# A fused attention and two-MoE kernel: 2 KB rows for keys and queries, z spread by halves of the rows, items of 592 slots, a new order list

## Chip, core and metric

The kernel runs on one core of a Trainium2 chip. The metric is the device time of one execution in microseconds (us). The times of the kernel before are 625.58, 625.61 and 626.13 us, median 625.61 us. A separate execution was profiled; the rows below are from it.

## What is computed

Three layers follow one another. The inputs are 4 batches of 8 heads, 576 tokens and 64 features a head, so 2304 tokens of 512 features, all in 4-byte floats.

```python
def phi(x):                                  # linear attention, 128 random features
    proj = np.einsum('bhsd,md->bhsm', x, omega)
    h = proj - np.sum(x * x, axis=-1, keepdims=True) / 2.0
    return np.exp(h - np.max(h, axis=-1, keepdims=True)) / np.sqrt(m)
kv = np.einsum('bhsm,bhsd->bhmd', k_p, v)
z = np.sum(k_p, axis=2)
x = np.einsum('bhsm,bhmd->bhsd', q_p, kv) / (np.einsum('bhsm,bhm->bhs', q_p, z)[..., None] + 1e-06)

h = x @ w_in                                 # layer two: softmax-gated unit, layer norm
solu = h * softmax(h)
x = (solu - mean) / np.sqrt(var + 1e-06) * g_ln @ w_out

e_idx = np.argmax(x @ w_gate, axis=1)        # layer three: one of 8 experts a token
for e in range(8):
    mask = e_idx == e
    ye = np.maximum(x[mask] @ w1[e], 0.0) @ w2[e]
    out[mask] = gate_w[mask, None] * eom[mask, e, None] * ye
```

## The kernel before, in words

A token tile is 128 tokens, so there are 18 tiles. Products that must be precise are made of three: each operand is split into an upper and a lower part, and `mm3` multiplies upper by upper, upper by lower and lower by upper (L162).

The first two layers are one long list of small steps, `ORDER`. Each entry is a step's name and its index, and `in_order` (L905) traces them one after the other and ties each instruction to the one before it on its engine. So the list fixes the order on PE, DVE, ACT, POOL and SP, and an engine that waits holds everything behind it. A second list, `LOADS`, gives the order of the loads on the SP queue; `pump` (L243) issues the next load as soon as its ring of buffers has room. The steps that matter here:

- `da` to `dl` turn a 512-column piece of `w_in` or `w_out`, stored in 8 bytes a number, into upper and lower parts: `db`, `dc`, `dd`, `de`, `df` on DVE, `dp` and `dg` on POOL, `dh` on ACT, and `dl` (L313) on DVE again, which takes the upper part from the number.
- `kp`, `kx`, `ke` are the projection of a key tile on PE, its maxima on DVE and its exponentials on ACT; `qp`, `qx`, `qe` are the same for queries. A projection holds two of the four half banks called `big` until its exponentials are done.
- `kv` and `kw` add a key tile to the sums of its batch. `vz` (L465) spreads the sums z of a batch over all partitions with four products, `zp`; `qz`, `qr` and `qs` divide by the denominators, `qz` and `qs` as long instructions on POOL.
- `ha`, `hb` (L162, tile `h`) are the products of the second layer, `u` and `l` (tile `x`) those with `w_out`; they need all of `dl`. `lo` (L643) stores a finished tile to DRAM (`x2d`).
- `wu` are products of ones with ones whose result nobody reads.
- `re`, `rg`, `rh` give each token a place in its expert's list, and `zb`, `zg`, `zt` pick and gather the first 256 tokens of the first expert. `zl` and `zm` (L869) load that expert's two weights on the SP queue, 2 MB each.

The third layer cuts each expert's tokens into items of at most `CAP` slots, in blocks of 128. Four items always run (`NSURE`); a fifth and more run only if the counts ask for them (`n_items`). `up` (L947) makes the hidden products (tile `hp`) with the slots as moving columns: 256 and then `CAP - 256` for the first item, two halves of `CAP // 2` for the others. `down` (L969) makes the output products (tile `yp`), 512 moving columns each, with up to 128 slots as the stationary side. Each block is scaled, scattered to `out_y` by POOL, and the next item's blocks are gathered and turned in between (`xpose`, L856).

Of the kernel before, what the change touches and what calls it, by code (L numbers as in the profile page):

```python
# [63 lines left out]
def slots(j):  # L64
# [15 lines left out]
    qe0 dc6 kv6 kv7 db7 dc7 dd7 dp0 ke11 dh0 dd6 de6 df6 dp11 vz0 dg11 de7 vy0 dl0 kp9 kx9 vt0 vd0 wu1 kp14 kx14 da3  # L80
    ke9 qz0 df7 kv8 vc1 qr0 db3 ke14 qp1 qx1 dc3 dp7 dh7 dl7 qe1 kv9 kv10 da8 dd3 de3 qp2 qx2 qs0 qz1 qr1 vz1 vy1 dp6
    kv11 qta0 qe2 qca0 qp5 qx5 dh6 vt1 gc2 gd2 db8 qs1 vd1 kp12 kx12 qe5 qtb0 qcb0 wu1 qta1 qtb1 dc8 nx0 qca1 qcb1
    kp13 ke12 ga3 kv12 dd8 de8 df8 gb3 kx13 ke13 qp4 qz2 qr2 dl6 qx4 dp8 dg8 kv13 gd1 df3 kp15 da4 db4 nx1 kx15 xh0
    dc4 dd4 de4 df4 vc2 qe4 kw13 kp16 kx16 ke15 xl0 xh1 ke16 qz5 kv14 kv15 ga0 kp17 gb0 dp3 dp4 vt2 kv16 dh4 qr5 vd2
    kx17 qp3 dl4 qx3 ke17 da5 db5 ha0 qs2 qz4 qr4 qe3 dh11 qta2 qca2 hxa0 qtb2 xl1 dh3 dl3 dc5 dd5 kv17 qcb2 da15 db15
    dc15 qs5 qta5 qca5 vz2 qz3 ha1 vy2 vc3 vt3 vd3 de5 df5 qr3 dp5 dd15 dh5 dl5 de15 df15 dp15 dg15 nx2 xh2 hxa1 hb1
    hxb1 da14 hb0 qs3 xl2 he1 ma1 hxb0 he0 mz1 ha2 ma0 mz0 dh8 qtb5 qcb5 qta3 qtb3 nx5 hxa2 qs4 dl8 db14 dc14 hb2 mb1
    da13 dd14 de14 hxb2 qca3 qcb3 qta4 nx3 xh5 qca4 he2 df14 dp14 dg14 xh3 xl5 qp6 ma2 qx6 qtb4 qcb4 qe6 db13 dc13
    dd13 de13 df13 ha5 mc1 qp7 qx7 qe7 mb0 hxa5 xl3 hb5 dl11 dp13 dg13 qz7 ta1 hxb5 gc0 gd0 tb1 da12 ca1 sa1 he5 dh14
    ma5 mz5 cb1 nx4 xh4 qp8 qx8 ga5 gb5 gc3 mb5 sb1 gd3 qe8 ta5 ga7 qr7 qs7 gb7 gc5 gd5 xl4 ta0 ca5 sa5 ca0 sa0 ga6  # L90
    gb6 tb5 cb5 sb5 mc5 gc7 qp9 qx9 dh15 qta7 qtb7 qca7 gc6 db12 dc12 dd12 de12 df12 qcb7 qz8 qr8 mc0 md0 ha4 dh13 qe9
    gd6 tb0 gd7 hb4 hxa4 hxb4 cb0 dp12 dg12 ga4 qz6 mz2 mb2 gb4 qr6 dh12 dl12 nx7 xh7 sb0 md1 he4 qs6 ma4 mz4 dl13 gc4
    me1 ha3 hxa3 mc2 qs8 gd4 hb3 hxb3 md5 qta6 qca6 qtb6 dl15 dl14 u1 xl7 he3 ma3 qcb6 nx6 xh6 xl6 qp11 qx11 mz3 ta2
    ca2 me0 mb4 sa2 qta8 qca8 qz9 qr9 ua1 l1 la1 lo1 mb3 ta3 qtb8 qcb8 u0 tb2 ub0 ub1 qe11 ca3 sa3 ua0 qs9 qp12 qx12
# [1085 lines left out]
```

## Time and profile before

| What | Value |
|---|---|
| median of 3 runs | 625.61 us |
| the profiled execution, its own time | 624.91 us |
| its span | 623.1 us |
| PE busy | 601.9 us (97%) |
| DVE busy | 359.5 us (58%) |
| ACT busy | 300.9 us (48%) |
| POOL busy | 236.7 us (38%) |
| HBM read, written | 44.70 MB, 9.70 MB |

PE is the engine of matrix products, DVE and ACT are the vector and scalar engines, POOL is GpSimd, and SP issues loads and stores. A share over the whole span is a mean over stages: DVE is nearly full in the first quarter and nearly idle in the last third. The profiled execution took 1.8 us more than its span, and 0.7 us less than the median.

### The profile page before, as it was taken

Reading aid. Unit: us, or ns where it says so; the run is one execution under the profiler, and the core shown is the slowest. Engines: PE = TensorE matmul, PEld = TensorE weight load, DVE = VectorE, ACT = ScalarE, POOL = GpSimd, SP = SyncE. Lnnn points to the kernel's source line nnn. Section 1 sums busy time; section 2 is a strip of 40 time slices with the busy share of each in tenths; the row PEclk is TensorE's granted clock in tenths of the full one; section 3 lists DMA queues with packets and bytes.
Section 4 is the critical chain, followed back from the end, with each engine's and each line's share of the span. In section 5 each row is a group of like instructions: output and inputs, shape, how many; then the busy total and the mean of one; then the engine's idle time right before and its main releaser. Section 6 shows DMA issues by size and latency. Waiting matters only on the chain.

```text
span 623.1 us, 12619 instructions
## 1 busy us (share of the span) xinstructions
PE 601.9 (97%) x5026; PEld 532.5 (85%) x5026; DVE 359.5 (58%) x952; ACT 300.9 (48%) x743; POOL 236.7 (38%) x169
## 2 busy tenths in 40 slices
PE   9999999998999999999999998999999999999994
PEld 8887888887988898988989897888798899879983
DVE  4998998999555364775676876864223123222200
ACT  5988985794653456345344423324333242325110
POOL 1435685558334226225201111173653182316011
PEclk9999999999999999999999999999999999999998
DMA  9986521210100001000004015066730433000010
GB/s 291 315 271 173 152 100 35 86 35 1 35 18 18 1 35 35 0 36 1 35 1 153 35 52 202 23 185 235 247 136 18 169 108 136 35 34 10 2 50 29
DMA packets 35077, 55.06 MB, mean 88 GB/s; under 512 B 2559, under 2 KB 21375, under 8 KB 35008
## 3 DMA queue, kind: packets, MB, share of 16 engines
q1 hardware_dynamic: 28384, 31.73, 15.6%
q0 software_dynamic: 6336, 22.29, 10.4%
q8 instruction: 42, 0.69, 0.5%
q14 instruction: 27, 0.22, 0.1%
q10 hardware_dynamic: 288, 0.13, 0.1%
HBM read 44.70 MB, written 9.70 MB: 87 GB/s over the span
## 4 chain that ended last, share of the span: by engine, by line
PE 71%; DVE 12%; issue 7%; DMA 6%; POOL 1%; ACT 1%; SPq 0%; POOLq 0%; DVEq 0%; ACTq 0%
PE x L162 14%; PE hp L162 14%; PE h L162 14%; PE yp L162 12%; PE qps L162 3%; PE qT L166 3%; PE lT L166 2%; PE kv L162 2%; PE xT L162 2%; DMA out_y<-y,idxs 2%; DVE kmx L374 1%; DVE w2l L150 1%; DMA xge<-x2d,idxe 1%; DMA kr<-in_kT 1%; PE xT L166 1%
## 5 line engine op out<-in xcount | busy, mean ns | idle before, releaser
L162 PE MATMUL x<-w2h,lth 128*128 128x256 f32 (+1 forms) x288 | 83.6, 290 | 0.8 <-DVE w2l L150 0.4
L162 PE MATMUL x<-w2l,lth 128*128 128x256 f32 (+1 forms) x288 | 82.0, 285 | 1.6 <-DVE w2l L150 1.6
L162 PE MATMUL x<-w2h,ltl 128*128 128x256 f32 (+1 forms) x288 | 81.9, 284 | 0.0
L958 DVE SCALAR_TENSOR_TENSOR htl<-hp,hth 128x304 fp32r<-128x304 f32 (+2 forms) x64 | 30.3, 474 | 82.7 <-ACT hth L957 68.9
L162 PE MATMUL hp<-xth,w1h 128*128 128x304 f32 (+1 forms) x224 | 68.6, 306 | 0.7 <-DVE htl L958 0.7
L162 PE MATMUL hp<-xtl,w1h 128*128 128x304 f32 (+1 forms) x224 | 68.4, 305 | 0.0
L162 PE MATMUL hp<-xth,w1l 128*128 128x304 f32 (+1 forms) x224 | 68.0, 304 | 0.0
L162 PE MATMUL yp<-w2h,hth 128*128 128x512 f32 (+1 forms) x160 | 64.1, 401 | 0.0
L162 PE MATMUL yp<-w2h,htl 128*128 128x512 f32 (+1 forms) x160 | 63.5, 397 | 0.0
L162 PE MATMUL yp<-w2l,hth 128*128 128x512 f32 (+1 forms) x160 | 63.4, 396 | 0.0
L479 POOL TENSOR_TENSOR pz<-qe,zb 128x1024 f32<-128x1024 f32 (+1 forms) x20 | 48.8, 2442 | 30.7 <-ACT qe L381 26.7
L957 ACT ACTIVATE hth<-hp 128x304 fp32r<-128x304 f32 (+2 forms) x64 | 27.2, 424 | 67.6 <-PE hp L162 67.6
L162 PE MATMUL h<-w1h,xth 128*128 128x512 f32 x144 | 58.9, 409 | 0.3 <-ACT qt L504 0.3
L162 PE MATMUL h<-w1h,xtl 128*128 128x512 f32 x144 | 57.0, 396 | 0.4 <-DVE xtl L150 0.4
L162 PE MATMUL h<-w1l,xth 128*128 128x512 f32 x144 | 56.9, 395 | 0.0
L162 PEld LDWEIGHTS x<-w2l,lth 128*128 128x128 f32 x288 | 54.2, 188 | 2.3 <-DVE w2l L150 1.8
L162 PEld LDWEIGHTS x<-w2h,lth 128*128 128x128 f32 x288 | 54.1, 188 | 2.1 <-ACT xo L153 0.8
L162 PEld LDWEIGHTS x<-w2h,ltl 128*128 128x128 f32 x288 | 54.3, 189 | 0.0
L150 DVE TENSOR_TENSOR xtl<-xT,xth 128x512 fp32r<-128x512 f32 (+1 forms) x36 | 24.2, 671 | 50.3 <-ACT xth L863 44.9
L981 POOL DMA_INDIRECT out_y<-y,idxs x20 | 20.1, 1006 | 77.1 <-ACT y L980 75.4
L490 POOL TENSOR_TENSOR qe<-qe,rd 128x1024 f32<-128x1024 f32 x18 | 34.4, 1916 | 35.6 <-DVE rd L486 28.3
L980 ACT ACTIVATE y<-yp,scs 128x512 f32<-128x512 f32 (+1 forms) x20 | 13.8, 688 | 70.3 <-PE yp L162 62.0
(210 smaller groups left out, 1468.6 us busy)
## 6 DMA issues: line engine op xcount, KB each, us to landing
raw<-in_w POOLq DMA_DIRECT2D x12, 1024.0 KB
v<-in_v SPq DMA_DIRECT2D x18, 260.0 KB, 4.7
kr<-in_kT SPq DMA_DIRECT2D x18, 256.0 KB, 5.9
qr<-in_qT SPq DMA_DIRECT2D x18, 256.0 KB, 3.1
x2d<-xo SPq DMA_DIRECT2D x18, 256.0 KB, 2.0
wout<-in_w_out SPq DMA_DIRECT2D x8, 512.0 KB, 4.9
win<-in_w_in SPq DMA_DIRECT2D x8, 512.0 KB, 6.1
raw<-in_w SPq DMA_DIRECT2D x4, 1024.0 KB, 6.2
```

What stands on the lines that cost most here:

```text
L150: return eng.tensor_tensor(out=out_, in0=a, in1=hi.bitcast(F32), op=ALU.subtract)
L162: return in_turn(nc.tensor.matmul(ps, **kw))
L166: return in_turn(nc.tensor.transpose(ps, x, ident[0:k, 0:k]))
L374: nc.vector.tensor_reduce(out=nmx[:, j, :], in_=of[kind, t][j], axis=AX.X, op=ALU.max, negate=True)
L479: nc.gpsimd.tensor_tensor(out=pz[r0:r1], in0=of["qe", t][r0:r1], in1=of["zb", b][r0:r1], op=ALU.mult)
L490: nc.gpsimd.tensor_tensor(out=e3, in0=e3, in1=of.pop(("rd", t)).to_broadcast([P, H, M]), op=ALU.mult)
L957: act = nc.scalar.activation(out=hi, in_=ps[:, 0:n], func=AF.Relu)
L958: dve = nc.vector.scalar_tensor_tensor(out=lo, in0=ps[:, 0:n], scalar=0.0, in1=hi.bitcast(F32), op0=ALU.max, op1=ALU.subtract)
L980: nc.scalar.activation(out=y, in_=ps, func=AF.Copy, scale=scs[0:k, col:col + 1])
L981: nc.gpsimd.indirect_dma_start(out=out, out_offset=bass.IndirectOffsetOnAxis(ap=idxs[0:k, col:col + 1], axis=0), in_=y, in_offset=None, bo ...
```

## The change

Six things change together.

1. Keys and queries are laid out by the host so that a tile is 128 rows of 2048 bytes. Before, a tile was 512 pieces of 512 bytes. Values lose their column of ones, which the sums took from an on-chip tile already: rows of 2048 bytes for 2080.
2. `vz` makes each of its four products from 64 partitions in place of 128, alternately from the lower and the upper half.
3. `CAP` is 592 for 608.
4. The threshold that moves a place into the next item, and the rounding of the place, are written so that they hold for 592.
5. The list `ORDER` is another one, with 2 entries of `wu` (13 products) for 9 entries (36 products).
6. The list `LOADS` is another one.

```diff
-CAP = 608
+CAP = 592
...
 LOADS = [(x[0], int(x[1:])) for x in """
-    k0 w9 k1 k2 w2 k6 k5 w1 v0 c0 w10 k8 k7 k3 v2 k10 q0 k4 v1 w0 w11 k9 v3 w7 v4 w3 q1 v5 w4 v6 w6 k11 k17 k12 v7 w8
+    k1 k0 w9 k4 k3 k2 v0 w10 v2 w2 k8 v1 c0 k6 c1 k10 v3 k9 w6 v4 q0 w3 k5 w11 w7 v5 q1 w0 v6 k11 w4 q5 w1 k7 k12 k14
...
 ORDER = """
-    wu9 wu5 kp0 kx0 da9 ke0 db9 dc9 da2 dd9 wu3 kp1 kx1 de9 df9 wu5 kp2 kx2 ke1 db2 dp9 dg9 ke2 dc2 wu6 kp6 dd2 kv0
+    da9 wu9 wu4 kp1 kx1 ke1 kp0 db9 dc9 kp2 kx0 ke0 kx2 ke2 dd9 da2 de9 da10 df9 kv0 dp9 kp4 kx4 ke4 kp3 kx3 ke3 db10
...
-                r = ap.tile([P, H, D + 1], F32, tag="va", name=f"v{t}", bufs=3)
-                nc.sync.dma_start(out=r, in_=v[t * P:(t + 1) * P])
+                r = ap.tile([P, H * D], F32, tag="va", name=f"v{t}", bufs=3)
             else:
                 r = raw2(f"{kind}r{t}")
-                src = qT if kind == "q" else kT
-                nc.sync.dma_start(out=r.rearrange("p (c t) -> p c t", c=NPAIR),
-                                  in_=src[:, :, t * P:(t + 1) * P].rearrange("c p t -> p c t"))
+            nc.sync.dma_start(out=r, in_=dict(v=v, q=qT, k=kT)[kind][t * P:(t + 1) * P])
+            if kind == "v":
+                r = r.rearrange("p (h d) -> p h d", h=H)
...
-            for i in range(4):
-                mm(pss[i // 2][:, i % 2], lhsT=ident[:, 32 * i:32 * i + 1].to_broadcast([P, P]), rhs=zk[:, b], start=True, stop=True)
+            for i in (0, 2, 1, 3):
+                rows = slice(i // 2 * D, i // 2 * D + D)
+                mm(pss[i // 2][:, i % 2], lhsT=ident[rows, 32 * i:32 * i + 1].to_broadcast([D, P]), rhs=zk[rows, b], start=True, stop=True)
...
-                V.scalar_tensor_tensor(out=place, in0=place, scalar=float(k * (CAP // SHORT + 1) - 1), in1=place,
+                V.scalar_tensor_tensor(out=place, in0=place, scalar=(k * CAP - 0.5) / SHORT + k - 1, in1=place,
...
-            V.tensor_scalar(out=pli, in0=place, scalar1=float(SHORT), scalar2=None, op0=ALU.mult)
+            V.tensor_scalar(out=pli, in0=place, scalar1=float(SHORT), scalar2=0.25, op0=ALU.mult, op1=ALU.add)
```

The lists move instructions on every engine. Three places follow.

The first is DVE's beginning, once the constants are made. `kmx` are the maxima of a key tile (two instructions a tile), `f` is a piece of weights under conversion. Before:

```order
L374 TENSOR_REDUCE kmx_162<-kps_0_150 128x4
L374 TENSOR_REDUCE kmx_162<-kps_1_151 128x4
L271 TENSOR_SCALAR f_165<-f_165 128x512
L276 TENSOR_SCALAR f_165<-f_165 128x512
L282 SCALAR_TENSOR_TENSOR f_165<-wout_113,f_165 128x512
L374 TENSOR_REDUCE kmx_198<-kps_0_184 128x4
L374 TENSOR_REDUCE kmx_198<-kps_1_185 128x4
L287 SCALAR_TENSOR_TENSOR f_165<-wout_113,f_165 128x512
```

Of the change:

```order
L372 TENSOR_REDUCE kmx_166<-kps_0_153 128x4
L372 TENSOR_REDUCE kmx_166<-kps_1_154 128x4
L270 TENSOR_SCALAR f_136<-f_136 128x512
L275 TENSOR_SCALAR f_136<-f_136 128x512
L372 TENSOR_REDUCE kmx_202<-kps_0_178 128x4
L372 TENSOR_REDUCE kmx_202<-kps_1_179 128x4
L372 TENSOR_REDUCE kmx_214<-kps_0_192 128x4
L372 TENSOR_REDUCE kmx_214<-kps_1_193 128x4
L281 SCALAR_TENSOR_TENSOR f_136<-wout_115,f_136 128x512
```

Three key tiles now stand ahead of the third step of the first piece of weights, where one stood.

The second is PE around the first `vz`, with the sums `kv` on one side and projections (`qps`, `kps`) on the other. Before:

```order
L162 MATMUL kv_1_624<-ke_649,v_670 32x128 x8
L162 MATMUL kv_1_624<-ke_649,ones 32x128 x4
L162 MATMUL zp_0_803<-zk,ident 128x256 x2
L162 MATMUL zp_1_804<-zk,ident 128x256 x2
L162 MATMUL kps_0_815<-bdr,kr_427 128x128
L162 MATMUL kps_1_816<-bdr,kr_427 128x128
```

Of the change:

```order
L161 MATMUL qps_0_539<-bdr,qr_359 128x128
L161 MATMUL qps_1_540<-bdr,qr_359 128x128
L161 MATMUL zp_0_560<-zk,ident 128x256
L161 MATMUL zp_1_561<-zk,ident 128x256
L161 MATMUL zp_0_560<-zk,ident 128x256
L161 MATMUL zp_1_561<-zk,ident 128x256
L161 MATMUL kv_0_568<-ke_277,v_357 32x128 x8
```

The two banks now take turns, as they do in a projection.

The third is the end of the SP queue: the second load of the first expert's weights (`raw`, two halves of `in_w2`) among the last stores of `x2d`. Before:

```order
L644 DMA x2d<-xo_4605 128x512
L644 DMA x2d<-xo_4852 128x512
L833 TENSOR_LOAD meta
L833 ISA x2
L837 ISA
L837 DMA raw_4364<-in_w 128x4x512
L837 ISA
L837 DMA raw_4364<-in_w 128x4x512
L644 DMA x2d<-xo_4972 128x512
L644 DMA x2d<-xo_4820 128x512
```

Of the change:

```order
L643 DMA x2d<-xo_4582 128x512
L832 TENSOR_LOAD meta
L832 ISA x2
L836 ISA
L836 DMA raw_4228<-in_w 128x4x512
L836 ISA
L836 DMA raw_4228<-in_w 128x4x512
L643 DMA x2d<-xo_4785 128x512
L643 DMA x2d<-xo_4683 128x512
L643 DMA x2d<-xo_5012 128x512
L643 DMA x2d<-xo_4861 128x512
```

Four stores, those of tiles 15, 12, 17 and 16, now stand behind the load, where two stood. In the list, the entry `zm0` stands ahead of six of the last products `l` and `u` (`l15 l12 u16 l16 u17 l17`), where it stood behind all of them; and ahead of the gathers `zg1 zg0` the product `l16` has moved in front of `zb0`, so that `u17` and `l17` are what is left behind it.

## Rows read from the trace of the kernel before

**Rows 1.** Stretches: us; busy PE, PEld, DVE, ACT, POOL; PEclk; DMA share; GB/s.

```profile
8.46:152.80 144.34, 140.16 (x1947) 119.27 (x1948) 135.10 (x267) 116.78 (x352) 84.66 (x51) 1.00 0.46 143
408.00:615.00 207.00, 206.34 (x1180) 182.58 (x1180) 53.01 (x98) 67.64 (x114) 80.26 (x60) 1.00 0.29 101
615.00:623.00 8.00, 0.17 (x1) 0.00 (x0) 0.00 (x0) 0.68 (x1) 0.92 (x1) 0.69 0.07 19
```

**Rows 2.** PE's waits: us in total, times, longest.

```profile
PE x L162 <- DVE w2l L150: 2.0, 2, 1.6
PE xTe L166 <- DMA xge<-x2d,idxe: 1.7, 1, 1.7
```

**Rows 3.** DVE in order of time: start, us, line, operation, count.

```profile
8.46 1.29 DVE L374 TENSOR_REDUCE kmx<-kps 128x4 f32<-128x512 f32 x2 [4.93 <-PE kps L162]
...
37.55 0.69 DVE L150 TENSOR_TENSOR w1l<-f,w1h 128x512 fp32r<-128x512 f32 x1
...
45.64 2.90 DVE L150 TENSOR_TENSOR w1l<-f,w1h 128x512 fp32r<-128x512 f32 x1
...
151.63 3.47 DVE L150 TENSOR_TENSOR w2l<-f,w2h 128x512 fp32r<-128x512 f32 x2
```

**Rows 4.** POOL in order of time.

```profile
45.49 2.50 POOL L479 TENSOR_TENSOR pz<-qe,zb 128x1024 f32<-128x1024 f32 x1 [3.83 <-DMA v<-in_v]
...
374.90 1.02 POOL L828 DMA_INDIRECT xge<-x2d,idxe  x1 [0.30 <-issue]
...
404.14 0.97 POOL L828 DMA_INDIRECT xg<-x2d,idxg  x1 [0.30 <-issue]
```

**Rows 5.** DVE's groups from 8.46 to 152.8: busy us, mean ns.

```profile
L271 DVE TENSOR_SCALAR f<-f 128x512 f32<-128x512 f32 x16 | 9.8, 610 | 0.0
L150 DVE TENSOR_TENSOR w1l<-f,w1h 128x512 fp32r<-128x512 f32 x8 | 9.3, 1162 | 0.7 <-ACT w1h L153 0.7
L276 DVE TENSOR_SCALAR f<-f 128x512 int32<-128x512 int32 x16 | 8.6, 545 | 0.3
L150 DVE TENSOR_TENSOR w2l<-f,w2h 128x512 fp32r<-128x512 f32 x7 | 8.3, 1191 | 0.0
L292 DVE TENSOR_SCALAR wout<-wout 128x512 int32<-128x512 int32 x8 | 3.4, 425 | 0.0
```

**Rows 6.** The chain that ended last, in order of time: start, us, what.

```profile
55.31 1.09 PE qps L162 x16
56.40 1.92 PE zp L162 x8
...
365.06 5.87 PE x L162 x48
...
374.90 7.17 DMA xge<-x2d,idxe
...
407.91 0.55 PE xT L166 x4
...
411.27 15.51 PE hp L162 x96
...
503.35 26.98 PE hp L162 x192
```

**Rows 7.** PE in order of time, at the start and at the gather.

```profile
1.17 6.17 PE L162 MATMUL kv<-ones 128*128 128x128 f32 x28 [1.17 <-DVE mhalf L197]
...
10.32 1.38 PE L162 MATMUL kv<-ones 128*128 128x128 f32 x10
...
371.64 0.28 PE L162 MATMUL x<-w2h,lth 128*128 128x256 f32 x1
```

**Rows 8.** ACT in order of time, at the start.

```profile
9.19 2.17 ACT L381 ACTIVATE ke<-kps,kmx 128x128 f32<-128x128 f32 x8 [2.56 <-DVE kmx L374]
```

**Rows 9.** ACT's waits up to 152.8: us in total, times, longest.

```profile
ACT f L266 <- DMA wout<-in_w_out: 2.9, 1, 2.9
```

**Rows 10.** SP in order of time, at the gather.

```profile
372.69 1.03 SPq L837 DMA_DIRECT2D raw<-in_w  x2
```

More of the change, by code (lines that the diff above doesn't have):

```diff
@@ L80 @@
[L80 to L94, printed above, removed]
@@ new lines @@
+    da0 kx9 dh11 kp11 ke9 kv7 kv8 kx11 ke11 ga3 gb3 dl6 vc1 qs0 da7 de1 df1 qz1 qr1 qp5 qx5 qe5 db0 dl11 kp14 kx14 dp1
+    da5 kv9 kv10 dc0 dd0 ke14 kv11 db7 db5 vt1 dc5 dd5 de5 dc7 qs1 qta1 vd1 df5 qtb1 de0 kp12 kx12 dd7 qca1 qcb1 dh1
+    dl1 vz1 de7 df7 vy1 dp5 ke12 dp7 nx1 qp2 qx2 da4 db4 qta0 qca0 dc4 dd4 kv12 kp13 qe2 qtb0 qcb0 df0 dp0 nx0 kx13
+    ke13 qp4 dh0 de4 kv13 vc2 qx4 qz2 df4 xh0 qe4 qr2 kp15 kx15 ke15 dp4 xl0 dl0 qz5 qr5 xh1 kw13 kv14 kp16 kx16 dh7
+    ke16 qs2 dh4 qp3 gc1 qx3 qe3 dl7 kv15 kv16 dl4 da3 kp17 kx17 ke17 qs5 xl1 qta2 ha0 qca2 qtb2 qcb2 db3 dc3 dd3 de3
@@ new lines @@
+    df3 hxa0 qz4 da8 db8 dc8 dd8 qta5 dp3 dh3 dl3 dh5 dl5 qca5 de8 df8 nx2 da15 dp8 dg8 qtb5 qcb5 qr4 ha1 hb1 hxa1 xh2
+    hxb1 xl2 hb0 he1 ma1 hxb0 qz3 qr3 gd1 da14 ha2 hb2 he0 mz1 qs4 ma0 qs3 qta3 qtb3 dh8 qca3 nx5 qcb3 xh5 db15 dc15
+    qta4 mz0 kv17 hxa2 hxb2 he2 qca4 dd15 de15 ma2 df15 mb0 qtb4 qcb4 vz2 vy2 qp6 xl5 qp7 mc0 qx6 nx3 qx7 qe6 qe7 gc3
+    db14 dc14 dd14 de14 ha5 dp15 df14 dg15 xh3 gd3 xl3 mz2 vt2 vd2 ga0 hxa5 mb1 qz7 ta1 md0 ga7 gb0 mc1 ca1 qr7 qs7
+    sa1 dp14 gb7 hb5 hxb5 qz6 tb1 nx4 cb1 sb1 he5 ma5 qta7 qca7 dh15 mz5 qtb7 qcb7 qp8 xh4 qx8 qr6 mb2 dl15 ta0 mb5
@@ new lines @@
+    xl4 ca0 qs6 nx7 xh7 xl7 me0 ha3 sa0 qe8 qp9 da13 db13 qx9 vc3 gc7 qe9 dc13 dd13 ha4 de13 df13 qta6 qtb6 dl8 da12
+    db12 dc12 dd12 gd7 de12 qca6 qcb6 gc0 dg14 ga6 gb6 hb4 gd0 df12 dp12 tb0 hxa4 hxb4 mc2 dg12 cb0 sb0 he4 ma4 gc6
+    dh12 nx6 xh6 ta2 ga4 hb3 gb4 xl6 gd6 ca2 tb2 sa2 dp13 dg13 dh13 dh14 cb2 ga5 hxa3 gc4 md1 qz8 gb5 mc5 gd4 dl14 ta5
+    ca5 dl12 dl13 me1 gc5 gd5 qr8 u0 hxb3 l0 sa5 he3 qs8 qta8 sb2 ua0 la0 ma3 qtb8 qca8 qcb8 qz9 qr9 qs9 vz3 qp10 qx10
+    vy3 qp11 zc0 qe10 u1 tb5 ub0 ub1 cb5 sb5 mz3 l1 mz4 md2 qx11 ua1 qe11 qta9 ha6 la1 qz10 qr10 qtb9 mb4 hb6 mb3 qz11
@@ L1158 @@
         "kT": pairs(k),
-        "v": np.concatenate([v.transpose(0, 2, 1, 3).reshape(NT, H, D), np.ones((NT, H, 1), f)], axis=2),
+        "v": np.ascontiguousarray(v.transpose(0, 2, 1, 3).reshape(NT, H * D)),
         "bd": bd,
```

56 lines of the change are left out of this document (28 added, 28 removed).

## The prediction
> **What bounds the kernel now.** I read the table of stretches first, then PE's waits, then DVE's groups. Three stretches have different limits.
>
> From 8.46 us to 152.8 us two engines are full: PE is busy 140.2 of 144.3 us and DVE 135.1, that is 97% and 94%, against 81% for ACT [rows 1]. Which of them gives the time is seen where the stretch ends. The first products with `w_out` start near 151 us, and the longest of PE's waits for DVE falls there: 2.0 us in two waits for `w2l`, the last lower part of `w_out` [rows 2]. PE had other products until then, DVE had nothing to spare. So in this stretch DVE is at least as much the bound as PE.
>
> DVE is slower there than its work asks. One `w1l` instruction takes 0.69 us at 37.55 and 2.90 us at 45.64; the second starts 0.15 us after a POOL instruction of 2.50 us and ends 0.55 us after it [rows 3, 4]. Two `w2l` at 151.63 take 3.47 us together [rows 3]. Against the undisturbed 0.69 us of an instruction with two inputs and the 0.425 us of one with one input [rows 3, 5], the groups have too much by 16 x (0.610 - 0.425) + 8 x (1.162 - 0.69) + 16 x (0.545 - 0.425) + 7 x (1.191 - 0.69) = 3.0 + 3.8 + 1.9 + 3.5 = 12.2 us [rows 5]. The Trainium skill, page "SBUF — State Buffer", states that a DVE instruction that uses the port pair shared with GpSimd, or has two inputs there while GpSimd reads, waits until GpSimd's whole instruction is over. The trace agrees: 2.90 us is the rest of POOL's 2.50 us and 0.55 us of its own.
>
> After that PE alone is the bound. In the third layer it is busy 206.3 of 207 us [rows 1], and every column taken from a product is time. Between, at the gather for the first expert, PE waits once for a transfer, 1.7 us [rows 2]. PE has finished by 615 us [rows 1], and the last scatter ends the span.
>
> **Items of 592.** PE's products of the hidden layer have 304 moving columns in 3 items, 2 halves x 8 x 4 x 3 = 192 each, and 352 in 96 of the first item. An item's 192 take 26.98 us, 0.1405 us each; the 96 take 15.51 us, 0.1616 each [rows 6]. A column costs (0.1616 - 0.1405) / 48 = 0.44 ns. The change takes 8 columns from 576 products and 16 from 96: (4608 + 1536) x 0.44 ns = **2.7 us** less. The output products keep their 512 moving columns, and a last block of 80 slots for 96 only narrows their stationary side: nothing, as the item's loop of gathers is hidden by PE's 99%. Bounds: nothing if a product under 304 columns stopped shrinking, 3.6 us by the mean price of a column (0.1405 / 304 = 0.46 ns; the rest from smaller transposes).
>
> This needs four items still. Run on the drawn inputs, the reference sends 561, 576, 591 and 576 tokens to four experts, and 591 is under 592 by one.
>
> **z by halves.** Four products on 128 rows take 1.92 us; sixteen instructions of a projection, which are on 64 rows by turns, have the same 2048 columns and take 1.09 us [rows 6]. So a `vz` costs about 1.09 us after, 0.83 us less, and four of them 3.3 us less. At worst the halves don't overlap, and it is nothing.
>
> **Fillers.** 23 products of ones, 46 instructions at 1.38 / 10 = 0.138 us [rows 7], leave the list, 6.3 us of PE's work. They stood where PE waited anyhow, so I count nothing but the first: one product of the first 14 goes, 2 x 6.17 / 28 = 0.44 us [rows 7], and the first projection starts that much earlier.
>
> **Loads.** A key tile's load has a quarter of the pieces. None of DVE's groups shown waits for a load [rows 5], and ACT waits once, 2.9 us, at the start [rows 9]. I take nothing; the bounds are 2.9 us less, and 2.9 us more if the first piece of weights, now third in the queue behind two key tiles, comes late.
>
> **The list, up to the first products with `w_out`.** On DVE the new list has the same steps ahead of them but for two `xl` more, one maximum and one lower part less, which cancel, and two small chains less (under 1 us). It has one step `nx` more on PE ahead of them, 1.0 us, so that much less is left behind. The beginning costs: DVE has three key tiles ahead of its third step of weights. The third projection needs a half bank that the first exponentials free. DVE is through the first two tiles' maxima and two conversions after 1.2 + 0.4 + 0.4 + 1.2 = 3.2 us, but the third projection can start only after 1.2 + 2.17 (the exponentials, [rows 8]) and its maxima 1.1 us later [rows 6], at 4.5 us: DVE stands 1.3 us. With the earlier start that is +0.9 us. If DVE sets the time: +0.9 - 1.0 (less PE work left behind) - 0.8 (the fourth `vz`, which stands behind in both lists) = 0.9 us less. If PE sets it: all four `vz` and the earlier start, 3.7 us less. I take the middle, **2.3 us** less for z, fillers and list, since both engines are over 94% busy [rows 1].
>
> **The gather.** The load of 2 MB for the first expert is issued at 372.69 [rows 10], just ahead of the gather at 374.90, whose data take 7.17 us [rows 4, 6]. A later gather, issued at 404.14 with no load beside it, had its data turned by PE at 407.91 at the latest, so 3.8 us [rows 4, 6]. In the new list the load stands ahead of six steps `l` or `u`, of which two take 5.87 us [rows 6]: some 17 us earlier, and done by then. But `l16` has moved ahead of the gather, and only two such steps and two short products, 6.3 us, are left for PE behind the last table product. That product ended at 371.64, when the next began [rows 7]; the gather needed 374.90 - 371.64 = 3.3 us to be issued and needs 3.8 to land, 7.1 us, so PE still waits 0.8 us in place of 1.7 [rows 2]: **0.9 us** less; bounds 0 and 1.7. The stores that are moved behind the load wait for their products anyhow; the one the gather needs, of tile 12, is ready two products ahead of it.
>
> **Sum.** 2.7 + 2.3 + 0.9 = 5.9 us less than the profiled execution's 624.9: 619.0. The median of the runs was 0.7 us above that execution, so I forecast a median of **619.7 us**.
>
> **Rivals.**
>
> - *The list meets POOL less often.* The 12.2 us of waiting on DVE are the largest reserve in its stretch. If the new list has half of it, DVE is 6 us faster and only PE's floor is left: the time is 613 to 614. For it: what collides is decided by the order alone, and hardly a step stands beside the same neighbours as before. Against it: the new list still has long POOL steps directly ahead of DVE steps that collide (`qz2 df4`, `qz4 db8`, `qs1 df5`, `qz8 dl14`). Chance 0.2.
> - *DVE hides the rest.* z and the gather bring nothing, and only the items are left, with the late beginning: 625.6 - 2.7 + 0.9 = 623.8. For it: the 2.0 us of waits for `w2l`. Chance 0.14.
> - *The port turns it round.* `qz8`, 2.44 us on POOL, stands just ahead of `dl14`, one of the last three lower parts that the first products wait for. A collision costs up to 2.90 - 0.69 = 2.2 us [rows 3]. Three more of them on the path eat the gain; five give 619.7 + 11 = 631. Chance 0.06.
> - *The clock.* The granted clock is full in every stretch while PE works, and 0.69 on average in the last 8 us, where PE has stopped [rows 1]. The first 28 fillers take 0.22 us each, later ones 0.138 [rows 7]. Without fillers PE stands idle between the first projections. The Trainium skill, page "TensorE: Matmul & The Clock Gate", section "Why this matters for your kernels", warns that gaps between bursts of products bring the half clock back. As a mechanism here: if PE ran at the price of the first fillers from 8.5 to 50 us, its useful work there, 97% of 41.5 us less 6.3 us of fillers, 34 us, would take 34 x 0.22 / 0.138 = 54 us: 12.7 us more, 632. Chance 0.03: DVE paces that stretch, and PE's gaps there should be 1 to 2 us.
> - *A fifth item.* If rounding on the chip gives the largest expert two tokens more than the reference, it has 593, and an item of some 57 us follows. Chance 0.01.
> - *Nothing to measure.* The parts cancel. Chance 0.05.
>
> **How the numbers follow.** My forecast has 0.51. A measurement of this kernel can tell 0.2% from no change, 1.3 us: same is 624.4 to 626.9. Faster: 0.51 + 0.2 + 0.14 = 0.85; same 0.05; slower 0.06 + 0.03 + 0.01 = 0.10. The range goes from 612, the first rival with a little more, to 625, past the second.
>
> **What would show it.** `zp` at 64 rows with 1.1 us a `vz`; 192 `hp` products in 26.3 us; the load `raw` ended when the gather is issued, and a wait of PE below 1 us there; DVE between 8.9 us and the first `x` product over 92% busy. I am wrong if the first `x` product comes before 145 us (the port), if it comes after 154, if the clock falls below full before 600 us, or if 25 scatters run for 20.

## The result and the profile after

The changed kernel takes 616.48 us, median of 4 runs (615.54 to 616.93); the kernel before, beside it, 625.60 (623.32 to 626.13). The ratio is 0.9858, 95% interval 0.9823 to 0.9894: **faster by 9.1 us**, where 5.9 were forecast. The profiled execution took 616.50 us, its span is 614.8 us. Medians in this text are over all runs; the ratios leave out the four runs that took over 1.5% more than the fastest of their kernel, one of e1's and three of the kernel before beside it.

The head of the page of the changed kernel, where a row of digits is the span in 40 slices:

```profile
PE 592.4 (96%) x4980; PEld 522.8 (85%) x4980; DVE 360.8 (59%) x952; ACT 299.3 (49%) x743; POOL 238.4 (39%) x169
...
PEclk9989999999999999999999999999999999999998
...
DMA packets 21251, 54.83 MB, mean 89 GB/s; under 512 B 2536, under 2 KB 2920, under 8 KB 21184
```

PE's busy time fell by 9.5 us, from 601.9. One slice ahead of the last has a clock under full; the kernel before had that only at the end.

PE's waits in the changed kernel (us in total, times, longest), the answer to [rows 2]:

```profile
PE hp L161 <- DVE htl L957: 2.2, 3, 1.0
PE kps L161 <- ACT ke L379: 1.6, 2, 1.1
PE kps L161 <- DMA kr<-in_kT: 1.3, 1, 1.3
...
PE xTe L165 <- ACT xo L152: 0.4, 1, 0.4
```

The two waits for `w2l`, 2.0 us, are not in it. Of the 1.7 us ahead of the gathered rows' transposes (`xTe`) 0.4 are left. New are the second and the third row, and most of the first (0.7 before).

The stretches (us; busy PE, PEld, DVE, ACT, POOL; PEclk; DMA share; GB/s), the answer to [rows 1]:

```profile
8.46:150.00 141.54, 135.37 (x1889) 113.42 (x1890) 129.44 (x255) 115.36 (x350) 81.32 (x48) 0.99 0.43 145
402.00:607.00 205.00, 202.98 (x1177) 178.26 (x1175) 51.88 (x97) 67.09 (x115) 80.27 (x60) 1.00 0.30 102
```

DVE is busy for 129.44 / 141.54 = 91% of the first stretch, after 94%. Its groups there, to be laid beside [rows 5] (busy us, mean ns, idle before):

```profile
L149 DVE TENSOR_TENSOR w1l<-f,w1h 128x512 fp32r<-128x512 f32 x8 | 10.1, 1282 | 0.0
L270 DVE TENSOR_SCALAR f<-f 128x512 f32<-128x512 f32 x16 | 9.5, 604 | 0.0
L275 DVE TENSOR_SCALAR f<-f 128x512 int32<-128x512 int32 x16 | 7.4, 465 | 0.4
L149 DVE TENSOR_TENSOR w2l<-f,w2h 128x512 fp32r<-128x512 f32 x7 | 4.8, 694 | 0.0
```

By the forecast's own formula the time lost beside POOL is now 16 x (0.604 - 0.425) + 8 x (1.282 - 0.69) + 16 x (0.465 - 0.425) + 7 x (0.694 - 0.69) = 2.9 + 4.7 + 0.6 + 0 = 8.2 us, against 12.2. All that `w2l` lost is gone; `w1l` loses more.

Three operations that the forecast had priced, in PE's timeline (a later `vz`, the gathered rows), POOL's (the gather) and SP's (the load of the first expert's second weights):

```profile
57.65 1.05 PE L161 MATMUL zp<-zk,ident 64*128 64x256 f32 x8
...
374.89 1.09 PE L165 MATMUL xTe<-ident,xge 128*128 128x128 f32 x8 [0.42 <-ACT xo L152]
```

```profile
369.09 1.30 POOL L827 DMA_INDIRECT xge<-x2d,idxe  x1 [15.39 <-DVE base L740]
370.69 1.02 POOL L827 DMA_INDIRECT xge<-x2d,idxe  x1 [0.30 <-issue]
```

```profile
349.33 0.98 SPq L836 DMA_DIRECT2D raw<-in_w  x2
```

A `vz` takes 1.05 us for 1.92 [rows 6]. The load is issued 20 us ahead of the gather, and the gather's last instruction is 4.2 us ahead of the first transpose, after 7.17 us [rows 6].

**Where the time went.** Four marks cut each trace into the same stretches: the first product `x` with `w_out`, the first `xTe`, the first hidden product of item 0's second part (at 411.1 in the kernel before, just ahead of the chain's `hp x96` [rows 6]), and the end of the span. The table has the marks' distances in us for every kernel of this text, each from one execution, between marks rounded to 0.1. "Half clock" are the stretches, up to 605 us, in which the granted clock was at 1.2 GHz.

| Kernel | to `x` | `x` to `xTe` | `xTe` to item 0's second part | to the end | span | half clock, us |
|---|---|---|---|---|---|---|
| before | 150.9 | 231.3 | 28.9 | 212.0 | 623.1 | none |
| changed | 149.9 | 225.0 | 29.8 | 210.1 | 614.8 | 36.0 to 39.4 |
| changed, again (e11) | 149.4 | 225.0 | 29.8 | 208.1 | 612.3 | none |
| e1 before, items | 150.2 | 230.7 | 28.7 | 207.8 | 617.4 | none |
| e2 before, z | 152.2 | 230.1 | 31.5 | 210.8 | 624.6 | 384.0 to 390.8 |
| e3 before, lists | 152.1 | 225.1 | 29.9 | 211.0 | 618.1 | 37.5 to 40.9 |
| e4 changed, old rows | 150.5 | 225.0 | 31.0 | 207.8 | 614.3 | 378.2 to 381.6 |
| e5 before, load earlier | 150.6 | 229.5 | 29.1 | 210.8 | 620.0 | none |
| e6 before, `dl` earlier | 151.5 | 229.0 | 29.3 | 210.7 | 620.5 | none |
| e7 changed, `dl` apart | 147.6 | 224.8 | 30.6 | 207.7 | 610.7 | 11.5 to 14.9, 376.7 to 380.1 |
| e8 changed, fillers more | 152.6 | 225.0 | 30.7 | 207.8 | 616.1 | 11.9 to 15.3, 39.2 to 42.6, 380.5 to 383.9 |
| e9 as e7, k5 earlier | 148.3 | 224.7 | 29.7 | 207.7 | 610.4 | 11.3 to 14.8 |
| e10 changed, old z | 151.8 | 225.3 | 29.9 | 208.0 | 615.0 | 26.8 to 30.2 |
| e12 as e7, old z | 150.3 | 224.9 | 29.9 | 207.9 | 613.0 | 11.4 to 14.8, 38.7 to 42.2 |

Between the two profiled executions of the first comparison, 1.0 us went ahead of the first `x`, 6.3 between it and the gather, and 1.9 behind; 0.9 were given back just behind the gather. Most of the gain lies between the first `x` and the gather, where the forecast's sum had named only the 0.9 us of the gather.

The two traces divide these 6.3 us. The stretch in the kernel before, then in the changed one (us; busy PE; PEclk; DMA share; GB/s):

```profile
150.92:382.20 231.28, 226.08 (x1716) 1.00 0.12 42
149.88:374.89 225.01, 222.55 (x1702) 1.00 0.12 43
```

PE has 3.5 us less work in it, and stands 2.7 us less. Of the work, one `nx` has moved ahead of the first `x`: its products, tile `xT`, are 176 there for 192, busy for 10.30 us and not 12.09. The fourth `vz` is 0.8 us shorter. Of the waits, the 2.0 us for `w2l` and 1.3 of the gather's 1.7 are gone, and so is one for `er` ahead of the products `tab`, which belong to the picking of tokens; two at the transposes of the second layer's rows (`lT`) are new or longer. Before, then of the change:

```profile
PE tab L162 <- DVE er L794: 0.8, 1, 0.8
```

```profile
PE lT L165 <- DVE s L564: 0.8, 1, 0.8
PE lT L165 <- DVE ltl L149: 0.7, 1, 0.7
```

### The profile page after: what moved, and what is told of

The parts are those of the page before. It is cut to its first block, busy times and chain, and to the rows that moved or that the text cites. A ratio compares the mean times of both kernels' runs of the same rounds, so it can differ in the third digit from the quotient of the medians.

```text
span 614.8 us, 12534 instructions
## 1 busy us (share of the span) xinstructions
PE 592.4 (96%) x4980; PEld 522.8 (85%) x4980; DVE 360.8 (59%) x952; ACT 299.3 (49%) x743; POOL 238.4 (39%) x169
## 2 busy tenths in 40 slices
DMA packets 21251, 54.83 MB, mean 89 GB/s; under 512 B 2536, under 2 KB 2920, under 8 KB 21184
## 5 line engine op out<-in xcount | busy, mean ns | idle before, releaser
L957 DVE SCALAR_TENSOR_TENSOR htl<-hp,hth 128x296 fp32r<-128x296 f32 (+2 forms) x64 | 29.8, 466 | 81.9 <-ACT hth L956 69.6
L161 PE MATMUL hp<-xth,w1h 128*128 128x296 f32 (+1 forms) x224 | 67.6, 302 | 1.8 <-DVE htl L957 1.8
L161 PE MATMUL hp<-xth,w1l 128*128 128x296 f32 (+1 forms) x224 | 67.7, 302 | 0.0
L161 PE MATMUL hp<-xtl,w1h 128*128 128x296 f32 (+1 forms) x224 | 67.3, 300 | 0.0
L956 ACT ACTIVATE hth<-hp 128x296 fp32r<-128x296 f32 (+2 forms) x64 | 26.7, 417 | 66.3 <-PE hp L161 66.2
L489 POOL TENSOR_TENSOR qe<-qe,rd 128x1024 f32<-128x1024 f32 x18 | 34.9, 1940 | 38.2 <-DVE rd L485 29.8
L577 POOL TENSOR_SCALAR s<-s,st 128x1024 f32<-128x1024 f32 x18 | 22.6, 1260 | 69.4 <-DVE st L573 30.1
```

Of the source, the lines that this page charges most:

```text
L489: nc.gpsimd.tensor_tensor(out=e3, in0=e3, in1=of.pop(("rd", t)).to_broadcast([P, H, M]), op=ALU.mult)
L577: nc.gpsimd.tensor_scalar(out=s, in0=s, scalar1=st[:, 10:11], scalar2=st[:, 11:12], op0=ALU.mult, op1=ALU.add)
L956: act = nc.scalar.activation(out=hi, in_=ps[:, 0:n], func=AF.Relu)
L957: dve = nc.vector.scalar_tensor_tensor(out=lo, in0=ps[:, 0:n], scalar=0.0, in1=hi.bitcast(F32), op0=ALU.max, op1=ALU.subtract)
```

## The experiments

My theory after this result: the items give what was forecast, the lists most of the rest, at the gather and in the second layer, and z little, because DVE holds the first stretch. The main rival: z and the shorter products give most, and the lists only move waits. The first four kernels have one part of the change each, or all but one.

**e1, the items alone.** On the kernel before:

```diff
-CAP = 608
+CAP = 592
...
-                V.scalar_tensor_tensor(out=place, in0=place, scalar=float(k * (CAP // SHORT + 1) - 1), in1=place,
+                V.scalar_tensor_tensor(out=place, in0=place, scalar=(k * CAP - 0.5) / SHORT + k - 1, in1=place,
...
-            V.tensor_scalar(out=pli, in0=place, scalar1=float(SHORT), scalar2=None, op0=ALU.mult)
+            V.tensor_scalar(out=pli, in0=place, scalar1=float(SHORT), scalar2=0.25, op0=ALU.mult, op1=ALU.add)
```

> The kernel before with items of 592 and the mended threshold, all else as before. By the price of a column (0.44 ns) the hidden products give 2.7 us and the time is 622.9. By the two traces the third layer, from the second part of the first item to the end of PE's work, went from 204.1 to 202.1 us, because a wait of PE for DVE of 1.27 us in the third item took the place of one of 0.25 us: 623.6. If that wait comes from the shorter products themselves it is seen here too (a start-to-start gap of over 1 us in the third item's hp); if it comes from where loads fall in the changed run, it is not, and the gain is 2.7.

Measured: 620.85 us (12 runs) beside 623.74, ratio 0.9953 (0.9923 to 0.9984), 2.9 us less. In the table the last stretch is 207.7 to 208.1 us in eight of the nine kernels with items of 592, and 210.7 to 211.0 in four of the five with 608: 3.0 us. The two exceptions are the first profiled executions of the kernel before (212.0) and of the changed one (210.1). The view of tile `hp` shows why the latter was long (ns, min/median/max; then the idle time):

```profile
L161 PE MATMUL hp<-xth,w1h x224: 295/299/404, 404.7 to 578.4; 128*128 128x296 f32 x96, 128*128 128x336 f32 x16
...
its engine sat idle before it (us, times) until:
  DVE htl L957: 1.8, 2
```

The same view of the same kernel in e11 has the product and no such wait:

```profile
L161 PE MATMUL hp<-xth,w1h x224: 295/299/325, 404.2 to 575.6; 128*128 128x296 f32 x96, 128*128 128x336 f32 x16
...
its engine sat idle before it (us, times) until:
who waited for it (us, times):
```

So those 1.8 us belong to one execution, and not to shorter products that run into ACT and DVE.

**e2, z by halves alone.** On the kernel before:

```diff
-            for i in range(4):
-                mm(pss[i // 2][:, i % 2], lhsT=ident[:, 32 * i:32 * i + 1].to_broadcast([P, P]), rhs=zk[:, b], start=True, stop=True)
+            for i in (0, 2, 1, 3):
+                rows = slice(i // 2 * D, i // 2 * D + D)
+                mm(pss[i // 2][:, i % 2], lhsT=ident[rows, 32 * i:32 * i + 1].to_broadcast([D, P]), rhs=zk[rows, b], start=True, stop=True)
```

> The kernel before with z spread by halves, all else as before. If PE sets the time at all four places, 3.3 us less: 622.3. If DVE sets it up to the first products with w_out, where three of the four stand, only the fourth counts, 0.8 us less: 624.8. In both cases a vz takes PE 0.9 to 1.1 us for 1.9.

Measured: 626.52 us (12 runs) beside 623.74, ratio 1.0053 (1.0012 to 1.0095): not faster, but slower by 0.5%. PE's waits from 100 to 400 us in its trace:

```profile
PE x L162 <- DVE w2l L150: 2.0, 2, 1.6
PE xTe L166 <- DMA xge<-x2d,idxe: 1.4, 1, 1.4
```

PE still waits 2.0 us for `w2l`, as in [rows 2], though its own products ahead are shorter: up to the first `x` PE is busy for 142.9 us where the kernel before has 145.6, and that product comes no sooner (152.2 for 150.9). DVE decided that end in the old list. Why the time is longer is seen in the granted clock. Behind the gather it was at half for 6.8 us in the profiled execution, and that stretch is 2.2 to 2.8 us longer than in the other four kernels with the old lists. Over whole runs the mean granted clock was 0.990 in the median of e2's twelve and 0.995 in that of the kernel before beside it. The seven runs of e2 at 0.988 to 0.992 took 625.4 us in the mean, the seven of the kernel before in the same range 625.8. So at a like clock z by halves is seen neither to cost nor to give anything here; whether its own waits lower the clock, no run shows.

**e3, the two lists alone.** On the kernel before:

```diff
 LOADS = [(x[0], int(x[1:])) for x in """
-    k0 w9 k1 k2 w2 k6 k5 w1 v0 c0 w10 k8 k7 k3 v2 k10 q0 k4 v1 w0 w11 k9 v3 w7 v4 w3 q1 v5 w4 v6 w6 k11 k17 k12 v7 w8
+    k1 k0 w9 k4 k3 k2 v0 w10 v2 w2 k8 v1 c0 k6 c1 k10 v3 k9 w6 v4 q0 w3 k5 w11 w7 v5 q1 w0 v6 k11 w4 q5 w1 k7 k12 k14
...
 ORDER = """
-    wu9 wu5 kp0 kx0 da9 ke0 db9 dc9 da2 dd9 wu3 kp1 kx1 de9 df9 wu5 kp2 kx2 ke1 db2 dp9 dg9 ke2 dc2 wu6 kp6 dd2 kv0
+    da9 wu9 wu4 kp1 kx1 ke1 kp0 db9 dc9 kp2 kx0 ke0 kx2 ke2 dd9 da2 de9 da10 df9 kv0 dp9 kp4 kx4 ke4 kp3 kx3 ke3 db10
...
```

> The kernel before with the two new lists alone: old rows, old z, items of 608. The forecast gave the list and the fillers about 0 up to the first x product and the gather 0.9 us: 624 to 625 if the parts add up. If the lists carry the surplus of the result over the forecast (3 us), 621 to 622. If the new list needs the 2 KB rows (it asks for 10.9 MB by 39 us where the old list asks for 10.8 MB by 41), the first 50 us grow by 2 us or more and the time is 625 or over.

Measured: 619.41 us (12 runs) beside 623.74, ratio 0.9936 (0.9907 to 0.9966): 4.3 us less by the medians, the largest single part. The first `x` comes no sooner, at 152.1, but from there to the gather it takes 225.1 us, as in every kernel with the new lists (224.7 to 225.3), against 229.0 to 231.3 with the old. So the lists alone bring what the stretch gained.

**e4, the changed kernel with the old rows** of keys, queries and values:

```diff
-                r = ap.tile([P, H * D], F32, tag="va", name=f"v{t}", bufs=3)
+                r = ap.tile([P, H, D + 1], F32, tag="va", name=f"v{t}", bufs=3)
+                nc.sync.dma_start(out=r, in_=v[t * P:(t + 1) * P])
...
+                src = qT if kind == "q" else kT
+                nc.sync.dma_start(out=r.rearrange("p (c t) -> p c t", c=NPAIR),
+                                  in_=src[:, :, t * P:(t + 1) * P].rearrange("c p t -> p c t"))
```

> The changed kernel with keys, queries and values laid out as before. The forecast counted the rows at nothing: 616.5. In the trace of the changed kernel PE waits 1.26 us for a key tile at 36 us and the clock falls for 3.4 us just then, so the loads are close to the bound there; if they are, 512-byte pieces make the wait longer and the time is 618 to 621.

Measured: 616.63 us (6 runs), ratio 0.9884 (0.984 to 0.9928). The changed kernel's own ratios are 0.9858 and, in e11, 0.9843. The rows of 2 KB are worth nothing to some 2.5 us; the intervals overlap, so this stays open. The granted clock of e4's runs is lower too, 0.990 in the median for 0.9935 in both sets of the changed kernel.

**e5, the load moved ahead of the gather.** In the kernel before the gather shares its time with the last part of a 2 MB load. DMA from 373 to 383 us there, queue by queue (packets, MB, share of 16 engines):

```profile
q1 hardware_dynamic: 1295, 2.54, 75.5%
q0 software_dynamic: 160, 0.52, 13.4%
```

The edit of the list, two places:

```diff
-    ... cb16 sb16 rb3 re3 ... ra5 la17 zm0 zt0 ...
+    ... cb16 sb16 zm0 rb3 re3 ... ra5 la17 zt0 ...
```

> The kernel before with one move: the raw load of the third layer's second half is issued some steps earlier in the second layer, behind step la17 of the list, now behind sb16. Theory (the gather stood behind that load in the queue): TensorE's wait of 1.7 us for the gathered rows goes, and the issue of the gather and the raw load no longer lie side by side; 1 to 1.7 us less than before, and a little more where the clock no longer falls there. Rival (the gather takes its 7 us whatever lies beside it): no change.

Measured: 621.39 us (12 runs) beside 623.27, ratio 0.9973 (0.9951 to 0.9996): 1.7 us less by the ratio, with an interval of 0.2 to 3.1 us. In PE's timeline the transposes follow without a wait, and in DMA from 373 to 380.5 us the gather (q0) is nearly alone:

```profile
380.12 1.39 PE L166 MATMUL xTe<-ident,xge 128*128 128x128 f32 x8
```

```profile
q0 software_dynamic: 160, 0.52, 26.7%
...
q1 hardware_dynamic: 6, 0.01, 0.4%
```

The theory holds in this: the load beside the gather cost the whole wait of [rows 2]. That the gather stood behind the load in one queue is not what the views show; they have two queues at work in the same stretch.

**e6, the lower parts earlier.** The last two `w2l` that the `x` products wait for, moved ahead in the old list:

```diff
-    ... gc6 db12 ... dl15 dl14 u1 ...
+    ... gc6 dl15 dl14 db12 ... u1 ...
```

> The kernel before with the lowering steps dl15 and dl14 of the weights moved ahead, from just before u1 to before db12. Theory (the two waits of the x products for w2l, 2.0 us each in a row, are what the list takes away): 2 to 4 us less in the stretch after the first x product, 1 to 2 us in the whole. Rival (VectorE is full until then, so what moves ahead delays the first x product by as much): no change.

Measured: 622.94 us (12 runs) beside 623.27, ratio 1.0003 (0.9976 to 1.003): nothing, within some 1.5 us. DVE's timeline shows that the edit did what it says; the pair took 3.47 us at 151.63 [rows 3]:

```profile
134.14 1.40 DVE L150 TENSOR_TENSOR w2l<-f,w2h 128x512 fp32r<-128x512 f32 x2
```

PE's wait there, and the DVE instruction that ends it:

```profile
PE x L162 <- DVE w2l L150: 1.0, 1, 1.0
```

```profile
151.23 0.17 DVE L150 TENSOR_TENSOR w2l<-wog,w2h 128x16 fp32r<-128x16 f32 x1
```

One wait of 1.0 us is left for 2.0. The pair's own wait, 1.6 us, is gone, but the first `x` also needs a short lower part of 16 columns, and that comes 0.5 us later on DVE than in the kernel before (150.69), although the pair, now ahead of it, ran 2.1 us faster. The first `x` is later by as much. In this one execution the gather's transposes come 1.7 us sooner all the same (table); the twelve runs show no gain. The medians fit the rival, that what moves ahead on a full DVE delays the rest, but the interval leaves room for the theory's 1 us.

**e7, two collisions taken away in the changed kernel.** In its trace the two longest `w1l`, on DVE, lie beside two instructions of POOL:

```profile
78.86 5.50 DVE L149 TENSOR_TENSOR w1l<-f,w1h 128x512 fp32r<-128x512 f32 x2
```

```profile
78.59 5.22 POOL L478 TENSOR_TENSOR pz<-qe,zb 64x1024 f32<-64x1024 f32 x2
```

The edit moves their entries in the list by a few places:

```diff
-    ... kp16 kx16 dh7 ke16 ... qe3 dl7 kv15 kv16 dl4 da3 kp17 kx17 ke17 qs5 xl1 qta2 ...
+    ... kp16 dh7 dl7 kx16 ke16 ... qe3 kv15 kv16 xl1 kp17 kx17 dl4 da3 ke17 qs5 qta2 ...
```

> The changed kernel with dl7 moved ahead of kx16, and xl1 and dl4 moved round kx17, so that the w1l lowerings at 78.9 and 81.5 us do not lie beside GpSimd's two instructions there, where each lost about 2 us. Theory (the port still costs TensorE time in the first stage): 1 to 2 us less than the changed kernel. Rival (TensorE sets the stretch by now, and what VectorE loses there is covered): no change.

Measured: 612.29 us (6 runs) beside 623.27, ratio 0.9831 (0.9803 to 0.9859). It is 3.8 us less than e8, which is the changed kernel with six filler products more (1.6 us of PE), on the same chip; the same order in e9, below, is 1.8 us less than the changed kernel beside it, by the medians of six runs each. The pair is now apart, and the group's mean is 772 ns for 1282:

```profile
76.18 0.64 DVE L149 TENSOR_TENSOR w1l<-f,w1h 128x512 fp32r<-128x512 f32 x1
...
83.06 0.89 DVE L149 TENSOR_TENSOR w1l<-f,w1h 128x512 fp32r<-128x512 f32 x1
...
L149 DVE TENSOR_TENSOR w1l<-f,w1h 128x512 fp32r<-128x512 f32 x8 | 6.1, 772 | 0.0
```

The first `x` comes at 147.6 us, 2.3 sooner than in the changed kernel's first trace and 1.8 sooner than in e11's. So DVE's lost time there is PE's time too: 5.50 - 0.64 - 0.89 = 4.0 us saved on DVE, about 2 on the whole. Here a collision was worth about half of the time that DVE lost. The edit also moves `kx16`, `kx17` and `xl1` by a few places, and no run separates that from the collision.

**e8, fillers meant for the wait** after which the clock fell. The new list has no `wu6` to move, so the edit adds six products of ones:

```diff
-    kp5 kx5 dp2 ...
+    wu6 kp5 kx5 dp2 ...
```

> The changed kernel with the filler products wu6 moved ahead of kp5, into TensorE's wait of 1.3 us for the fifth group of key rows, after which the granted clock was at half for 3.4 us. Theory (that wait is what lets the clock fall): full clock there, 0.5 to 1.7 us less than the changed kernel. Rival (fillers take the place of useful products, and the clock falls elsewhere): no change, or 0.5 us more.

Measured: 616.06 us (6 runs) beside 623.27, ratio 0.9886 (0.9859 to 0.9912): no gain. The stretches at half clock in its trace:

```profile
11.90:15.30 3.40, 3.40 (x51) 2.88 (x51) 2.50 (x5) 3.40 (x13) 0.78 (x1) 0.50 1.00 358
39.20:42.60 3.40, 3.40 (x36) 3.18 (x35) 2.12 (x6) 1.78 (x6) 1.59 (x1) 0.50 0.15 29
380.50:383.90 3.40, 3.30 (x15) 3.30 (x16) 1.62 (x11) 0.75 (x3) 0.00 (x0) 0.50 0.00 0
```

The clock fell at the same place of the program, and at two more. But the theory was not put to the test. The wait of 1.3 us in the changed kernel is not at `kp5`. The list begins with `kp1 kp0 kp2 kp4 kp3 kp8 kp6 kp10 kp5 kp7`, other steps left out; in the changed kernel's trace the ninth projection, `kp5`, starts at 31.92 without a wait, and it is the tenth, `kp7`, that waits. In e8 the fillers, then the projections of key tiles 5 and 7:

```profile
33.09 1.61 PE L161 MATMUL kv<-ones 128*128 128x128 f32 x12
34.63 1.16 PE L161 MATMUL kps<-bdr,kr 64*128 64x128 f32 x16
...
38.99 1.95 PE L161 MATMUL kps<-bdr,kr 64*128 64x128 f32 x16 [1.81 <-ACT ke L379]
```

The fillers ran in front of useful work, and PE still stood 1.8 us at `kp7`, just ahead of the fall at 39.2. Fillers inside that wait remain untried.

**e9, the load of key tile 5 earlier**, on e7:

```diff
-    ... w6 v4 q0 w3 k5 w11 ...
+    ... w6 v4 k5 q0 w3 w11 ...
```

> The kernel of e7 with one load moved: the fifth group of key rows is asked for two places earlier, ahead of q0 and w3. Theory (TensorE's wait of 1.1 us for these rows at 36.7 us is on the path to the first x product): 0.5 to 1.1 us less than e7. Rival (q0 or w3 come later by as much and something waits for them): no change.

Measured: 612.49 us (6 runs) beside 623.72, ratio 0.9814 (0.9783 to 0.9845), as e7. PE's waits up to 85 us still have the rows of keys:

```profile
PE kps L161 <- DMA kr<-in_kT: 3.2, 2, 2.1
```

The longer of the two is at the third projection, at 10 us, for a load that the edit leaves in its place. The other is at the tenth; the projections of tiles 5 and 7:

```profile
33.38 1.16 PE L161 MATMUL kps<-bdr,kr 64*128 64x128 f32 x16
...
37.28 1.16 PE L161 MATMUL kps<-bdr,kr 64*128 64x128 f32 x16 [1.04 <-DMA kr<-in_kT]
```

So the edit moved the load of a tile that PE did not wait for, and the wait for tile 7 is 1.0 us, as in e7 (1.1). The run decides neither for the theory nor for the rival; an earlier `k7` remains untried. With e7 it is the fastest version here by the medians.

**e10, the changed kernel with the old z**, e2's diff backwards.

> The changed kernel with the old z: all 128 rows again, 8 products of 256 columns one after another, everything else as changed. Theory (z saves nothing in the old lists, where VectorE sets the first stretch, but about 2 us in the new ones): 1.5 to 2.5 us more than the changed kernel, first x product 1 to 2.5 us later. Rival (z is covered in the new lists too, and the parts simply add): within 0.5 us of the changed kernel.

**e11, the changed kernel again**, on the same chip, with no edit.

> The changed kernel itself, beside the two others on the same chip, so that a difference of 1 or 2 us to it can be read. Theory and rival alike: 616 to 617 us. If the half clock of 3.4 us falls at one place in one execution and at another in the next, its trace shows other stretches at half clock than 36.0 to 39.4 us; if the program sets the place, the same.

Measured: e10 614.61 us (614.22 to 616.7, 6 runs), ratio 0.9846 (0.9816 to 0.9876); e11 614.32 (612.89 to 616.12, 6 runs), ratio 0.9843 (0.9811 to 0.9874), both beside 623.72. By the medians z is worth 0.3 us, against the theory's 1.5 to 2.5; the intervals, 0.003 each way, are too wide to rule that out. The two traces say otherwise: the first `x` comes 2.4 us later with the old z, and the span is 2.7 us longer. But e10's profiled execution was the longest of its six, 616.7 us, and has a stretch of half clock that e11's has not. In e11 the clock stayed full where the first execution had it at half; the row of the first, then that of e11:

```profile
36.00:39.40 3.40, 3.35 (x31) 3.38 (x32) 1.27 (x3) 2.24 (x8) 3.40 (x2) 0.50 0.10 8
```

```profile
36.00:39.40 3.40, 3.19 (x72) 2.88 (x73) 2.67 (x6) 3.40 (x13) 3.40 (x2) 1.00 0.49 127
```

So the place of the half clock is not set by the program alone. In e11 PE waited 0.3 us, not 1.3, for that key tile.

**e12, e7 with the old z**, the same edit once more.

> The kernel of e7 (the two w1l lowerings moved away from GpSimd's instructions) with the old z of 128 rows. Theory (z's shorter products show little in the changed kernel because VectorE's lost time at 79 to 84 us holds the first stretch there; with that gone TensorE sets it and its 3.6 us of fewer products count): 2 to 3.5 us more than e7, a ratio to the kernel before of 0.986 to 0.989. Rival (something else holds the first stretch, such as ScalarE's copies, and z stays covered): within 0.7 us of e7, a ratio of 0.982 to 0.984.

Measured: 614.95 us (611.49 to 615.39, 6 runs) beside 625.56, ratio 0.9829 (0.9789 to 0.9868); e7's was 0.9831. By the ratios z is covered here too; by the times themselves it is worth 2.7 us, but on another chip than e7, where the kernel before also took 2.3 us more. The trace has its first `x` 2.0 to 2.7 us later than e7 and e9. Runs at a like granted clock lean to a gain, though they are few: five of e12 at 0.991 or 0.992 took 615.0 us in the mean, three of e7 at 0.990 to 0.993 took 612.3; two of e10 at 0.996 or 0.997 took 614.2, two of e11 at 0.996 took 613.4. **Undecided**: what z saves in the new lists lies between nothing and 2.7 us, and no run here separates it from what one execution differs from the next.

## Why the prediction was right, and where it was not

The direction and the range held; the size was 3.2 us short of what was measured. That it was not further off is partly luck: what was put too high ahead of the first `x` made up for part of what was left out behind it. Term by term:

- **Items, 2.7 us.** Right: 2.9 us alone (e1), and 3.0 us in the last stretch over the kernels of the table. The bounds 0 and 3.6 were not needed. Four items still run: the scatters `out_y` are 20.
- **z, fillers and list up to the first `x`, 2.3 us, the middle between 0.9 ("DVE sets the time") and 3.7 ("PE sets it").** Oversized. The first `x` came 1.0 us sooner, and 1.5 in e11. With the lists alone (e3) it came 1.2 later. The price of a `vz` was right, 1.05 us against 1.09 expected; what failed was to count half of it as path. In the old list it brings nothing (e2), in the new list between nothing and 2.7 us (e10, e12).
- **The gather, 0.9 us.** The mechanism was right, the size a little short: PE's wait went from 1.7 to 0.4, so 1.3 us. The load beside it cost the whole wait: in e5, with no other edit, it is gone. The forecast had added 3.3 us to the issue and 3.8 to land, and set 6.3 us of PE's work against it, so a rest of 0.8; the wait that remained is 0.4.
- **What stood at nothing: PE's other waits between the first `x` and the gather.** This is the step that failed. The forecast read the 2.0 us of waits for `w2l` as the mark of DVE's bound and put nothing in the sum for their going. Behind the first `x` it had only the gather and, in the case that DVE sets the time, 1.8 us for one `nx` and the fourth `vz`. The stretch took 6.3 us less: 3.5 us of PE's work, of which those two are most (the `nx` 1.8, the `vz` 0.8), and 2.7 us of standing, of which the gather is 1.3; the waits for `w2l` (2.0) and at `tab` (0.8) went too, and those at `lT`, 0.3 before and 1.7 now, took some back. The lower parts take 0.69 us each now, not 1.19. e3 shows that the lists do this; which of their entries, no run separates. e6, with two of them moved alone, keeps 1.0 of the 2.0 us.
- **Loads, nothing.** Between nothing and 2.5 us (e4): within the bounds of 2.9, not decided.

Of the rivals, *the list meets POOL less often* happened by a third: 8.2 us lost for 12.2, where the rival wanted half and 6 us of time. It counted a microsecond of DVE as one of time; e7 has about half of that, 4.0 us less lost on DVE for some 2 us. *DVE hides the rest* was the truth about z in the old list and not about the whole. *The port turns it round* named `dl14`; in the new list no `w2l` loses anything, and it was two `w1l` ahead of that which did. *The clock* was named as a sign of error, a fall below full before 600 us, and that sign came. But 3.4 us at half clock are no 12.7 us: behind the gather, where the table has kernels with and without it, such a stretch costs 30.6 to 31.0 less 29.7 to 29.9, so 0.7 to 1.3 us. It did not turn the result.

The signs: `zp` at 1.05 us, 192 `hp` products in 26.0 us (e11; 26.3 forecast), the load done before the gather and PE's wait there below 1 us came as written. DVE was busy for 91% of the stretch where over 92% was asked.

Together, the parts' ratios give 0.9936 for the lists and 0.9953 for the items, so 0.989 by their product; the changed kernel has 0.9858 and 0.9843. The 2 to 3 us between are z, the rows, or their meeting with the lists; the intervals of 0.003 each way don't tell which.

## What to carry to other kernels

A stretch with two full engines pays neither of them in full: four `vz` shorter by 0.87 us each, 3.5 us, brought between nothing and 2.7 us, and 4.0 us of DVE's stalls about 2. Follow the effect of a new order past the next meeting point of the engines, since most of this one's gain lay behind the product at which the forecast stopped. And a transfer that is waited for should not be issued behind a large load that nobody needs yet; moving one entry of the list was worth 1.7 us (0.2 to 3.1). Before an edit is aimed at a wait, find in the list which step it is: e8 and e9 missed theirs by one key tile.

## What was not expected of the hardware

- The granted clock fell to half for 3.4 us, once for 6.8, in nine of the fourteen traces, though PE was busy within these stretches (3.35 of 3.40 us in the changed kernel). What PE did before: in the changed kernel it had waited 1.3 us for a key tile, and in e12, the longest, 2.7 us for the same tile. But waits of 2.6 and 2.4 us at 11 us in e3 and e4 brought no fall, and the three waits of 0.4, 0.7 and 0.8 us at the gather stand alike in the traces of the changed kernel, of e4 and of e7, and the clock fell behind them only in the last two. The Trainium skill, page "TensorE: Matmul & The Clock Gate", section "Why this matters for your kernels", lays the half clock to gaps between bursts of products. These rows agree that it comes behind waits, and show that the same waits bring it in one execution and not in another.
- Two POOL instructions on 64 partitions took 5.22 us, one on 128 partitions with the same 1024 columns 2.50 us [rows 4]: half the partitions didn't make them shorter.
- The DMA packets fell from 35077 to 21251 with the rows of 2 KB, and no run here shows a gain in time that is larger than its interval.
